# A gated recurrence and a gated linear unit on one core: roots of the first chunks on VectorE, decay constants by a series, and a new order of the queues

## The chip, the core and the metric

The kernel runs on one core of a Trainium2 chip. The core has five engines that run their own queues of instructions: TensorE (PE; its weight loads are shown as PEld), VectorE (DVE), ScalarE (ACT), GpSimd (POOL) and SyncE (SP), which here issues nearly all DMA transfers. The metric is the time of one execution on the device, in microseconds (us).

## The reference

Inputs `x`, `r_gate` and `i_gate` have the shape (4, 6336, 256). First comes a gated linear recurrence along the 6336 steps of each of 4 sequences, then a gated linear unit with a causal convolution of 5 taps:

```python
a_base = sigmoid(a_param)                                   # 256 values
a_t = exp(8 * sigmoid(r_gate) * log(clip(a_base, 1e-6, 1 - 1e-6)))
norm = sqrt(maximum(1 - a_t * a_t, 1e-6))
x_gated = norm * sigmoid(i_gate) * x
h = a_t[:, t] * h + x_gated[:, t]                           # for every t; y[:, t] = h
gate = sigmoid(sum over k of conv_w[k] * y shifted by 4 - k)
out = (gate * (y @ w_val)) @ w_out
```

## The kernel before

The 25,344 rows are cut into 51 windows of 512 rows (the first two and the last have 256), and the windows into 28 chunks: chunks 0, 1 and 2 are single windows of 256, 256 and 512 rows, chunks 3 to 25 have two windows of 512, the last two are single again. Everything is unrolled in Python. Nothing is scheduled by a compiler: a string, `ORDER`, lists some 980 steps, and each step appends its instructions to the queues of its engines in that order. A step is a name with a window or chunk number, a half of the 256 columns where it has one, and PSUM banks after `@`. Within one engine the instructions run in the order of the string; between engines semaphores make an instruction wait for its data and for its buffers.

The steps of the recurrence, by chunk `c`, half `h` or window `w`:

- `lr.w`, `li.w`, `lx.w`: SP issues the load of a window of `r_gate`, `i_gate` or `x` into a ring of four windows. A load waits until the step that reads the old content of its place is done.
- `ta.c`, `tb.c`: ACT takes tanh of half the gate (a sigmoid is taken as half of one plus tanh), into `taring` and `tbring`.
- `tr.c.h`: PE transposes the tangents of `r_gate` to PSUM; `ex.c.h`: ACT takes the exponential with scale and bias from `khf`, 128 x 2 constants worked out at the start, and writes the decays to `aring`. From chunk 3 on one `tr` and one `ex` do two chunks.
- `sq.c.h`: POOL squares the decays into `ering` (`sa` does the same on ACT for a few).
- `rt.b.k`: ACT takes the root of a quarter less a quarter of the square, for a batch `b` of chunks, as bfloat16 in place. The root is in another set of ACT's tables than tanh and exp, so a batch is framed by two table loads.
- `pp.w`, `up.w`: POOL adds one to the tangent of the input gate and multiplies by `x`, into `uring`. For a few windows `xp.w` (PE copies `x` to PSUM) and `uv.w` (DVE does both in one operation) take their place.
- `nt.c`: PE transposes the roots' packed words; `xg.c`: DVE multiplies them with `uring`; `xt.c.h`: PE transposes the product; `sc.c.h`: DVE scans, with the decays from `aring`, into `yring`.

The steps of the second layer, by window: `cv.w` (PE, the convolution as products with diagonal matrices), `tg.w` (ACT, tanh for its gate), `vl.w` (PE, product with `w_val`), `gv.w` (DVE, gate times value), `ou.w` (PE, product with `w_out`), `cd.w` or `ca.w` (copy from PSUM by DVE or ACT), `st.w` (SP, store).

Ahead of them stand `s_ident` (an identity matrix), `s_small` (loads of `a_param` and `conv_w`), `s_kt` (the constants `khf`), `s_diag` (the diagonal matrices), and among them `s_wl` and `s_wcast` (the weights). In `s_kt` ACT takes an exponential, DVE makes the clipped sigmoid of it in three operations (lines 228 to 230), ACT takes its logarithm (line 232), loads another set of tables (line 233), and DVE multiplies by four (line 234). The tables with the logarithm are loaded first of all (line 185).

The lists that the change touches besides: `BATCHES` says which chunks' roots are taken together, and the dispatch loop loads a set of tables where a step needs another one than is loaded:

```python
table, have = {"ta": EXP, "tb": EXP, "tg": EXP, "ex": EXP, "rt": SQRT}, EXP
for word in ORDER.split():
    ...
    if table.get(name, have) != have:
        have = table[name]
        nc.scalar.preload_act_table_set(have)
    emit[name](*[int(k) for k in idx], *[int(k) for k in at.split(",") if k])
```

Of the kernel before, what the change touches and what calls it, by code (L numbers as in the profile page):

```python
# [8 lines left out]
P = 128  # L9
CONV_K = 5  # L10
FP32 = mybir.dt.float32
BF16 = mybir.dt.bfloat16
ACT = mybir.ActivationFunctionType
ALU = mybir.AluOpType
# [4 lines left out]
BATCHES = [[0, 1, 2], [3, 4], [5, 6, 7, 8], [9, 10, 11, 12], [13, 14, 15, 16], [17, 18, 19, 20], [21, 22, 23, 24], [25,  # L19
    26, 27]]  # L20
# [21 lines left out]
s_ident s_small s_kt s_diag lr.1 lr.0 lr.2 lr.3 li.0 ta.0 ta.1 lr.4 tr.0.1@0 tr.0.0@7 ex.0.1 lr.5 tr.1.0@3 ta.2 ex.1.0  # L42
lr.6 tr.2.0@2 ex.0.0 li.2 sq.1.0 ex.2.0 tr.1.1@7 li.1 tr.2.1@6 ex.1.1 lx.0 tb.0 s_wl.1 ta.3 li.4 pp.0 li.3 sq.0.1 lx.1
sq.2.0 ex.2.1 lr.7 ta.4 lr.8 lx.2 tb.2 tr.3.0@0,1 s_wl.3 up.0 lr.10 tb.1 sq.2.1 ex.3.0 tr.3.1@6,7 lx.3 sq.0.0 lx.4
ex.3.1 sq.3.0 s_wl.2 s_wl.0 tb.3 sq.1.1 xp.1@7 sq.4.0 ta.5 li.8 uv.1 lr.9 sq.4.1 li.5 li.6 xp.2@4,5 sq.3.1 uv.2 rt.0.0
lx.6 pp.3 li.7 rt.1.0 lr.12 nt.1@2 pp.4 nt.0@7 xg.1 xg.0 xt.0.0@6 up.4 xt.0.1@1 nt.2@7 sc.0.0 xt.1.0@2 xt.1.1@4 sc.0.1
xg.2 up.3 lx.8 sc.1.1 nt.3@6,7 lx.5 sc.1.0 lr.11 xt.2.0@4 ta.6 cv.1@2,3 sc.2.0 s_wcast cv.0@0,1 xg.3 xt.2.1@4 tg.0
lr.14 tb.4 lr.13 sc.2.1 xt.3.0@7 lx.7 vl.0@0,1 gv.0 tb.5 li.10 pp.6 sc.3.0 tr.5.0@0,1 up.6 tg.1 ex.5.0 vl.1@4,5 gv.1
pp.5 tr.5.1@6,7 sq.5.0 ou.0.0@4 ex.5.1 cv.2@2,3 cd.0.0 st.0 xt.3.1@4 up.5 li.11 tg.2 li.12 sc.3.1 vl.2@0,1 li.9 ta.7
ou.1.0@3 pp.7 nt.4@6,7 cd.1.0 cv.3@4,5 ta.8 up.7 xg.4 st.1 lx.9 lx.10 gv.2 tg.3 tr.7.1@2,3 lr.18 sq.5.1 xt.4.1@7 lr.15  # L50
ex.7.1 xt.4.0@6 lr.16 sc.4.1 tr.7.0@0,1 sq.6.1 cv.4@4,5 ex.7.0 sc.4.0 sq.7.1 xp.8@2,3 tg.4 lx.12 lx.11 tb.6 uv.8
vl.4@0,1 sq.8.0 ou.2.0@4,5 gv.4 cv.5@6,7 tb.7 li.14 sq.6.0 lr.17 cd.2.0 li.13 vl.5@2,3 tg.5 li.15 sq.8.1 li.16 xp.9@0,1
gv.5 st.2 uv.9 sq.7.0 rt.2.0 ou.4.0@2,3 cd.4.0 ou.5.0@4,5 pp.11 cd.5.0 xp.10@6,7 up.11 lx.14 uv.10 lx.13 rt.2.1
vl.3@2,3 gv.3 nt.5@4,5 pp.12 lx.15 xg.5 nt.6@0,1 up.12 xg.6 xt.5.0@7 xt.5.1@2 sc.5.0 cv.6@4,5 tb.8 ou.3.0@0,1 ta.10
li.18 cd.3.0 pp.13 pp.14 sc.5.1 ta.9 lr.22 nt.7@0,1 up.14 lr.21 xt.6.1@7 tb.9 sc.6.1 lr.19 tr.9.0@2,3 lr.20 up.13 li.17
lx.16 tg.6 st.3 xg.7 vl.6@6,7 li.19 ex.9.0 pp.15 li.20 tr.9.1@4,5 gv.6 st.4 xt.6.0@0 up.15 xt.7.0@1 sc.6.0 ex.9.1
ou.6.0@2,3 pp.16 ta.12 cv.7@4,5 sc.7.0 sq.10.0 cv.9@6,7 tg.7 lr.25 st.5 sq.9.1 cd.6.0 tg.9 lx.18 nt.8@0,1 lr.26 ta.11
xg.8 vl.7@4,5 up.16 xt.7.1@7 gv.7 cv.8@2,3 tb.10 lr.24 lr.23 sc.7.1 sq.9.0 lx.20 ou.7.0@0,1 tg.8 tr.11.0@4,5 ex.11.0
pp.18 cd.7.0 vl.8@6,7 cv.10@2,3 sq.10.1 gv.8 st.7 li.22 tg.10 st.6 vl.9@0,1 lx.17 pp.17 tb.11 gv.9 ou.8.0@6,7
tr.11.1@4,5 cd.8.0 xt.8.0@1 ex.11.1 pp.19 sc.8.0 st.8 ou.9.0@2,3 lx.19 sq.11.0 cv.12@6,7 li.21 ta.14 xt.8.1@4 sq.11.1  # L60
sc.8.1 cv.11@0,1 tg.12 tg.11 up.18 cd.9.0 ta.13 vl.11@4,5 gv.11 vl.10@6,7 pp.20 lx.22 lr.30 vl.12@0,1 gv.10 sq.12.0
li.24 lr.27 rt.3.0 gv.12 lr.28 ou.11.0@6,7 sq.12.1 cd.11.0 ou.10.0@0,1 cd.10.0 ou.12.0@2,3 up.17 rt.3.1 cd.12.0
nt.9@6,7 xg.9 up.19 lx.21 nt.10@0,1 lr.29 xg.10 li.23 xt.9.0@5 st.10 st.9 up.20 sc.9.0 st.11 nt.11@6,7 xt.10.1@0 tb.12
tr.13.1@2,3 xg.11 xt.9.1@1 cv.13@4,5 ex.13.1 li.25 pp.22 sc.9.1 li.26 up.22 vl.13@6,7 tg.13 sc.10.1 cv.15@2,3 ta.15
sq.13.1 cv.14@4,5 tg.15 lr.31 gv.13 lr.32 pp.21 tg.14 vl.15@0,1 lx.24 gv.15 sq.14.1 vl.14@2,3 tb.13 tr.13.0@6,7 gv.14
# [43 lines left out]
def kernel(  # L109
# [30 lines left out]
    clen = [sum(CHUNKS[c]) for c in range(NCH)]  # L140
# [5 lines left out]
    e_at = SQUARES_AT  # L146
# [35 lines left out]
    live = {}  # L182
# [391 lines left out]
```

## Time and profile before

| | before |
|---|---|
| time, median of 3 runs (us) | 285.6 (285.45 to 285.82) |
| time of the profiled execution (us) | 285.77 |
| its span, first to last instruction (us) | 284.0 |
| granted clock of TensorE, mean | 0.985 |
| ACT, DVE, PE, POOL busy (us) | 270.3, 245.4, 240.4, 235.3 |
| moved by DMA | 104.75 MB, 369 GB/s over the span |

The time of an execution holds 1.8 us outside of the span. In the profile a row of a group has the busy time in us, the mean length of one instruction in ns, and the idle time of the engine just before the group with what ended most of it. A row of the timeline begins with its start and length in us; an arrow in brackets names the idle time before it and the releaser. L366 is line 366 of the kernel.

### The profile page before, as it was taken

What the parts mean: (1) busy time and instruction counts of PE and PEld (TensorE: products, weight loads), DVE (VectorE), ACT (ScalarE), POOL (GpSimd) and SP (SyncE); (2) the same over time, 40 slices, a digit from 0 to 9 for tenths busy, and PEclk for the clock granted to TensorE, in tenths of its full rate; (3) what the DMA queues carried; (4) which work ended last, traced back from release to release, by engine and by line L of the source; (5) the groups of instructions that cost most, each with busy time, mean ns of one, the idle gap of its engine ahead of it and who ended that gap; (6) DMA issues with size and microseconds to landing.
All of it is one profiled execution on the core that took longest, in us unless ns stands there. A gap on an engine that the chain in (4) does not pass through costs nothing.

```text
span 284.0 us, 6202 instructions
## 1 busy us (share of the span) xinstructions
PE 240.4 (85%) x2468; PEld 163.3 (58%) x2491; DVE 245.4 (86%) x203; ACT 270.3 (95%) x192; POOL 235.3 (83%) x157
## 2 busy tenths in 40 slices
PE   2247779997789889999898998899998989999993
PEld 1232556555656557584476584666774756856662
DVE  2002887989999999999999999999999999999981
ACT  6899999999999999999999999999999999998763
POOL 1369989997999998999999999998998997993200
PEclk9995999999999999999999999999999999999998
DMA  7999999999999999999999999999999999772646
GB/s 235 360 401 377 408 410 412 408 411 404 313 387 420 416 419 409 414 414 413 418 420 414 412 413 412 417 413 415 411 321 366 392 420 364 277 259 108 250 178 247
DMA packets 29995, 104.75 MB, mean 369 GB/s; under 512 B 3335, under 2 KB 3854, under 8 KB 29966
## 3 DMA queue, kind: packets, MB, share of 16 engines
q1 hardware_dynamic: 29952, 104.35, 94.0%
q8 instruction: 19, 0.31, 0.4%
q14 instruction: 10, 0.08, 0.1%
q10 hardware_dynamic: 14, 0.01, 0.0%
HBM read 78.39 MB, written 25.95 MB: 367 GB/s over the span
## 4 chain that ended last, share of the span: by engine, by line
ACT 29%; PE 19%; POOL 18%; DMA 11%; DVE 11%; issue 10%; SPq 0%; ACTq 0%; DVEq 0%; POOLq 0%
POOL ering L366 8%; DVE yring L463 7%; ACT taring L295 7%; ACT aring L358 7%; POOL uring L317 7%; ACT tbring L298 6%; PE banks L475 6%; PE banks L490 5%; DMA iring<-in_i_gate_dram 5%; DMA xring<-in_x_dram 4%; ACT tgring L482 4%; PE banks L505 3%; POOL tbring L305 3%; ACT oring L515 3%; DMA rring<-in_r_gate_dram 2%
## 5 line engine op out<-in xcount | busy, mean ns | idle before, releaser
L366 POOL TENSOR_TENSOR ering<-aring 128x1024 f32<-128x1024 f32 (+2 forms) x54 | 91.0, 1705 | 11.5 <-ACT aring L358 11.3
L463 DVE TENSOR_TENSOR_SCAN yring<-aring,yring,banks 128x1024 bf16<-128x1024 f32 (+5 forms) x48 | 98.4, 2060 | 2.2 <-PE banks L430 1.9
L317 POOL TENSOR_TENSOR uring<-tbring,xring 128x1024 bf16<-128x1024 bf16 (+1 forms) x46 | 96.7, 2115 | 4.3 <-DMA xring<-in_x_dram 3.3
L475 PE MATMUL banks<-yring,diag 64*64 64x512 bf16 (+7 forms) x1080 | 62.6, 361 | 2.5 <-ACT aring L358 0.9
L495 DVE SCALAR_TENSOR_TENSOR tgring<-tgring,banks 128x1024 bf16<-128x1024 bf16 (+1 forms) x51 | 59.1, 1178 | 4.8 <-PE banks L490 2.3
L305 POOL TENSOR_SCALAR tbring<-tbring 128x1024 bf16<-128x1024 bf16 (+1 forms) x46 | 46.9, 1030 | 17.2 <-ACT tbring L298 17.2
L505 PE MATMUL banks<-wo,tgring 128*128 128x256 bf16 x396 | 51.5, 273 | 5.1 <-DVE tgring L495 2.9
L490 PE MATMUL banks<-yring,wv 128*128 128x512 bf16 (+4 forms) x193 | 48.4, 359 | 6.1 <-DVE yring L463 2.5
L358 ACT ACTIVATE aring<-banks,khf 128x2048 f32<-128x2048 bf16 (+3 forms) x34 | 53.2, 1605 | 0.0
L505 PEld LDWEIGHTS <-tgring 128*128 128x128 bf16 x396 | 42.0, 114 | 17.0 <-issue 10.0
L482 ACT ACTIVATE tgring<-banks 128x1024 bf16<-128x1024 f32 (+1 forms) x51 | 50.6, 1009 | 0.9 <-PE banks L475 0.7
L295 ACT ACTIVATE taring<-rring 128x2048 bf16<-128x2048 f32 (+2 forms) x28 | 47.9, 1723 | 1.7 <-DMA rring<-in_r_gate_dram 1.6
L298 ACT ACTIVATE tbring<-iring 128x2048 bf16<-128x2048 f32 (+2 forms) x28 | 48.0, 1724 | 0.0
L391 ACT ACTIVATE ering<-ering 128x4096 bf16<-128x4096 f32 (+2 forms) x14 | 44.4, 3216 | 0.1
L475 PEld LDWEIGHTS <-diag 64*64 64x64 bf16 x1080 | 28.6, 106 | 25.8 <-issue 10.8
L513 DVE COPY oring<-banks 128x1024 f32<-128x1024 f32 (+1 forms) x34 | 39.7, 1180 | 0.9 <-PE banks L505 0.9
L342 PE MATMUL banks<-ident_b,taring 128*128 128x128 bf16 x396 | 30.0, 230 | 12.0 <-ACT taring L295 9.5
L342 PEld LDWEIGHTS <-taring 128*128 128x128 bf16 x396 | 25.9, 103 | 16.8 <-ACT taring L295 11.0
L490 PEld LDWEIGHTS <-wv 128*128 128x128 bf16 x216 | 19.7, 97 | 26.2 <-issue 12.7
L430 PE MATMUL banks<-ident,uring 128*128 128x128 f32 x198 | 30.0, 279 | 3.2 <-DVE uring L416 1.7
L405 PE MATMUL banks<-ident,ering 128*128 128x128 f32 x184 | 26.8, 292 | 3.3 <-ACT ering L391 1.8
L416 DVE TENSOR_TENSOR uring<-banks,uring 128x2048 bf16<-128x2048 bf16 (+2 forms) x25 | 27.9, 1128 | 0.8 <-PE banks L405 0.3
(39 smaller groups left out, 135.4 us busy)
## 6 DMA issues: line engine op xcount, KB each, us to landing
rring<-in_r_gate_dram SPq DMA_DIRECT2D x48, 512.0 KB, 8.9
iring<-in_i_gate_dram SPq DMA_DIRECT2D x48, 512.0 KB, 9.5
xring<-in_x_dram SPq DMA_DIRECT2D x48, 512.0 KB, 9.0
out_dram<-oring SPq DMA_DIRECT2D x48, 512.0 KB, 9.5
rring<-in_r_gate_dram SPq DMA_DIRECT2D x3, 256.0 KB, 3.2
iring<-in_i_gate_dram SPq DMA_DIRECT2D x3, 256.0 KB, 7.3
xring<-in_x_dram SPq DMA_DIRECT2D x3, 256.0 KB, 7.7
out_dram<-oring SPq DMA_DIRECT2D x3, 256.0 KB, 3.9
```

The costliest lines, as they stand in the source:

```text
L295: nc.scalar.activation(**tangent(c, taring, NTR, rring, NRI))
L298: nc.scalar.activation(**tangent(c, tbring, NTI, iring, NII))
L317: nc.gpsimd.tensor_tensor(out=u, in0=t1, in1=xt, op=ALU.mult)
L342: nc.tensor.transpose(out=bank[:, o:o + P], in_=taring[:, place(w, NTR), j, h * P:(h + 1) * P], identity=ident_b[:])
L358: nc.scalar.activation(out=dst, in_=src, func=ACT.Exp, scale=khf[:, h:h + 1], bias=khf[:, h:h + 1])
L366: nc.gpsimd.tensor_tensor(out=e, in0=a, in1=a, op=ALU.mult)
L463: nc.vector.tensor_tensor_scan(out=yring[:, h, col:col + o1 - o0], data0=aring[:, h, a_at[c] + o0:a_at[c] + o1], data1=xT[:, o0:o1], initi ...
L475: nc.tensor.matmul(out=gp[oh * 64:oh * 64 + 64, h, a:b], lhsT=diag[half * 64:half * 64 + 64, h, k, :], rhs=yring[half * 64:half * 64 + 64, ...
L482: nc.scalar.activation(out=tgring[:, w % NTG, :, 0:wins[w]], in_=live.pop(("gp", w))[:, :, 0:wins[w]], func=ACT.Tanh, scale=0.5)
L490: nc.tensor.matmul(out=val[:, m, a:b], lhsT=wv[:, hk, m * P:(m + 1) * P], rhs=yring[:, hk, col:col + b - a], start=(hk == 0), stop=(hk == ...
L495: nc.vector.scalar_tensor_tensor(out=tgring[:, w % NTG, :, 0:wins[w]], in0=tgring[:, w % NTG, :, 0:wins[w]], scalar=1.0, in1=live.pop(("va ...
L505: nc.tensor.matmul(out=ops[:, j * D:(j + 1) * D], lhsT=gv[:, hk, j:wins[w]:J], rhs=wo[:, hk, :], start=(hk == 0), stop=(hk == H - 1))
```

## The change

Three things are changed.

The roots of chunks 0 and 1 are no longer taken by ACT. A new step `rd` takes each by seven operations of VectorE on 512 fp32 values a partition (both halves of a chunk): it subtracts one, gets a first estimate of the inverse root by arithmetic on the bits, and corrects it with a polynomial. Its scratch is in two places of `oring` that are not used before the first outputs. `BATCHES` has chunks 0, 1 and 2 as batches of their own; chunk 2 stays with ACT, right before the batch of chunks 3 and 4.

The constants `khf` are worked out without a logarithm: one exponential on ACT, and a series for the logarithm in VectorE operations on 128 x 2 values. The first set of tables is the one with exp, and the second load of tables in `s_kt` is gone.

`ORDER` is new as a whole. It has the same steps but for these: `rd.0.0` and `rd.1.0` are added and the first batch's `rt` has chunk 2 alone; windows 3 and 6 go by `xp` and `uv` instead of `pp` and `up`, window 9 by `pp` and `up` instead of `xp` and `uv`; the copy of window 46 is on DVE instead of ACT; ACT squares other halves of chunks (22.1 and 27.1 instead of 22.0 and 26.0), POOL the ones left.

```diff
-BATCHES = [[0, 1, 2], [3, 4], [5, 6, 7, 8], [9, 10, 11, 12], [13, 14, 15, 16], [17, 18, 19, 20], [21, 22, 23, 24], [25,
-    26, 27]]
+BATCHES = [[0], [1], [2], [3, 4], [5, 6, 7, 8], [9, 10, 11, 12], [13, 14, 15, 16], [17, 18, 19, 20], [21, 22, 23, 24],
+    [25, 26, 27]]
...
-        nc.scalar.preload_act_table_set("natural_log_exp_and_others")
+        nc.scalar.preload_act_table_set("exp_and_others")
...
-            nc.scalar.activation(out=ksig[:], in_=kps[:, 0:H], func=ACT.Exp, scale=-1.0)
-            nc.vector.tensor_scalar(out=ksig[:], in0=ksig[:], scalar1=1.0, scalar2=None, op0=ALU.add)
-            nc.vector.reciprocal(out=ksig[:], in_=ksig[:])
-            nc.vector.tensor_scalar(out=ksig[:], in0=ksig[:], scalar1=1e-6, scalar2=1.0 - 1e-6,
+            low, p, z, q = kcol[:, 0], kcol[:, 1], kcol[:, 2], kcol[:, 3]
+            nc.vector.tensor_scalar(out=low, in0=kps[:, 0:H], scalar1=0.0, scalar2=4.0, op0=ALU.min, op1=ALU.mult)
+            nc.vector.scalar_tensor_tensor(out=p, in0=low, scalar=0.5, in1=kps[:, 0:H], op0=ALU.mult, op1=ALU.subtract)
+            nc.scalar.activation(out=p, in_=p, func=ACT.Exp)
+            nc.vector.tensor_scalar(out=z, in0=p, scalar1=2.0, scalar2=None, op0=ALU.add)
+            nc.vector.reciprocal(out=z, in_=z)
+            nc.vector.tensor_tensor(out=z, in0=z, in1=p, op=ALU.mult)
+            nc.vector.tensor_tensor(out=p, in0=z, in1=z, op=ALU.mult)
+            nc.vector.tensor_scalar(out=q, in0=p, scalar1=1.0 / 15, scalar2=None, op0=ALU.mult)
+            for k in (13, 11, 9, 7, 5, 3):
+                nc.vector.scalar_tensor_tensor(out=q, in0=q, scalar=1.0 / k, in1=p, op0=ALU.add, op1=ALU.mult)
+            nc.vector.scalar_tensor_tensor(out=q, in0=q, scalar=1.0, in1=z, op0=ALU.add, op1=ALU.mult)
+            nc.vector.scalar_tensor_tensor(out=q, in0=q, scalar=-8.0, in1=low, op0=ALU.mult, op1=ALU.add)
+            nc.vector.tensor_scalar(out=khf[:], in0=q, scalar1=4.0 * math.log(1e-6), scalar2=4.0 * math.log1p(-1e-6),
                                     op0=ALU.max, op1=ALU.min)
-            nc.scalar.activation(out=ksig[:], in_=ksig[:], func=ACT.Ln)
-            nc.scalar.preload_act_table_set("exp_and_others")
-            nc.vector.tensor_scalar(out=khf[:], in0=ksig[:], scalar1=4.0, scalar2=None, op0=ALU.mult)
...
+        def op_rd(b, k):
+            cs = root_pieces(b)[k]
+            o = e_at[cs[0]]
+            n = H * (e_at[cs[-1]] + clen[cs[-1]] - o)
+            v = ering[:, H * o:H * o + n]
+            y, s = (oring[:, 1].rearrange("p j d -> p (j d)")[:, j * 512:j * 512 + n] for j in range(2))
+            q = oring[:, 2].rearrange("p j d -> p (j d)")[:, 0:n]
+            nc.vector.tensor_scalar(out=v, in0=v, scalar1=-1.0, scalar2=-1e-6, op0=ALU.add, op1=ALU.min)
+            nc.vector.tensor_scalar(out=y.bitcast(I32), in0=v.bitcast(I32), scalar1=-0.5,
+                                    scalar2=float(0x5f3759df - 2 ** 30), op0=ALU.mult, op1=ALU.add)
+            nc.vector.scalar_tensor_tensor(out=s, in0=v, scalar=-5.0 / 32, in1=y, op0=ALU.mult, op1=ALU.mult)
+            nc.vector.scalar_tensor_tensor(out=y, in0=s, scalar=-32.0 / 5, in1=y, op0=ALU.mult, op1=ALU.mult)
+            nc.vector.scalar_tensor_tensor(out=q, in0=y, scalar=4.2, in1=y, op0=ALU.add, op1=ALU.mult)
+            nc.vector.scalar_tensor_tensor(out=q, in0=q, scalar=7.0, in1=y, op0=ALU.add, op1=ALU.mult)
+            nc.vector.scalar_tensor_tensor(out=ering[:].bitcast(BF16)[:, 4 * o:4 * o + n], in0=q, scalar=7.0, in1=s,
+                                           op0=ALU.add, op1=ALU.mult)
...
```

The new order's first lines, up to the roots of chunks 3 and 4 and the first gate:

```
s_ident s_small s_kt s_diag lr.0 lr.1 lr.2 lr.3 li.0 li.1 ta.0 lr.4 tr.0.0@1 ex.0.0 ta.1 ta.2 lr.5 tr.1.1@5 tr.1.0@1
ex.1.1 lr.6 tr.2.0@2 ex.1.0 tr.2.1@3 li.2 ex.2.0 sq.1.0 li.3 ex.2.1 lx.0 sq.1.1 tr.0.1@2 lx.1 tb.0 rd.1.0 ex.0.1 li.4
pp.0 ta.3 sq.0.1 sq.0.0 sq.2.0 tb.1 lr.7 ta.4 lr.8 sq.2.1 lx.2 s_wl.3 rd.0.0 lx.3 tb.2 tr.3.1@2,3 s_wl.2 up.0 s_wl.1
ex.3.1 tr.3.0@4,5 lx.4 ex.3.0 sq.4.1 lr.9 nt.0@6 xp.1@7 lr.10 tb.3 sq.4.0 nt.1@0 uv.1 li.6 xg.0 s_wl.0 xg.1 ta.5
xt.0.0@4 xt.0.1@7 sq.3.0 xt.1.0@0 xt.1.1@5 sc.0.1 li.5 sc.0.0 xp.2@6,7 lx.6 sc.1.0 sq.3.1 li.7 uv.2 lx.5 rt.2.0
xp.3@2,3 pp.4 rt.3.0 nt.2@1 li.8 up.4 xg.2 sc.1.1 lr.11 xt.2.1@6 cv.0@0,1 uv.3 lr.12 s_wcast sc.2.1 nt.3@4,5 tg.0 xg.3
ta.6 ...
```

128 lines of the change are left out of this document (63 added, 65 removed).

## The prediction

> **What bounds the kernel now.** I read the page's busy times and slices first, then ScalarE's waits, then the start of the timeline.
>
> ```profile
> PE 240.4 (85%) x2468; PEld 163.3 (58%) x2491; DVE 245.4 (86%) x203; ACT 270.3 (95%) x192; POOL 235.3 (83%) x157
> DVE  2002887989999999999999999999999999999981
> ACT  6899999999999999999999999999999999998763
> POOL 1369989997999998999999999998998997993200
> ```
> ```profile
> ACT oring L515 <- PE banks L505: 5.9, 5, 2.0
> ACT taring L295 <- DMA rring<-in_r_gate_dram: 1.6, 1, 1.6
> ```
> ```profile
> 264.21 1.01 ACT L515 COPY oring<-banks 128x1024 f32<-128x1024 f32 x1 [1.98 <-PE banks L505]
> ```
>
> ACT is busy for 270.3 of 284.0 us. Its one wait for a load, 1.6 us, is at the start; its 5.9 us on PE's output products begin with the 1.98 us before 264.21. Between them it runs without a pause, so every microsecond by which ACT starts its main stretch later, or waits inside it, is a microsecond of time. DVE and POOL have their free time at the front, where the change puts its new work. So the start decides:
>
> ```profile
> 2.65 0.17 DVE L228 TENSOR_SCALAR ksig<-ksig 128x2 f32<-128x2 f32 x1 [2.65 <-ACT ksig L227]
> 2.85 0.17 DVE L229 RECIPROCAL ksig<-ksig 128x2 f32<-128x2 f32 x1
> 3.47 1.28 ACT L233 ACT_TABLE_LOAD   x1
> 4.77 1.15 ACT L295 ACTIVATE taring<-rring 128x512 bf16<-128x512 f32 x2
> 8.03 1.06 ACT L295 ACTIVATE taring<-rring 128x1024 bf16<-128x1024 f32 x1 [1.57 <-DMA rring<-in_r_gate_dram]
> 16.72 1.17 POOL L317 TENSOR_TENSOR uring<-tbring,xring 128x512 bf16<-128x512 bf16 x1 [2.80 <-DMA xring<-in_x_dram]
> 17.40 3.99 ACT L358 ACTIVATE aring<-banks,khf 128x2048 f32<-128x2048 bf16 x2
> ```
> ```profile
> 19.52 8.02 POOL L366 TENSOR_TENSOR ering<-aring 128x1024 f32<-128x1024 f32 x5
> 22.60 0.73 DVE L331 SCALAR_TENSOR_TENSOR uring<-tbring,banks 128x512 bf16<-128x512 bf16 x1 [17.58 <-PE banks L322]
> 25.00 1.28 ACT L542 ACT_TABLE_LOAD   x1
> 26.30 5.42 ACT L391 ACTIVATE ering<-ering 128x2048 bf16<-128x2048 f32 x2
> 30.33 1.26 DVE L463 TENSOR_TENSOR_SCAN yring<-aring,banks 128x256 bf16<-128x256 f32 x2 [0.41 <-PE banks L430]
> 33.03 1.91 ACT L295 ACTIVATE taring<-rring 128x2048 bf16<-128x2048 f32 x1
> ```
>
> The reader is to see: ACT leaves the load-bound part at 8.03, runs the first squares' inputs until 21.4, roots from 26.30, and is back from its tables at 33.03. DVE rests for 17.58 us before 22.60. POOL's squares end at 27.54, just ahead of the second root (28.11: the pair began at 26.30, the first takes 1.91).
>
> **Constants by a series.** What goes is one table load (1.28) and one logarithm. What comes is two small VectorE steps ahead of the exponential and fourteen behind it, each starting 0.20 after the last (2.65 to 2.85), so khf is ready at about 5.9 instead of 3.66. ACT's first exp now waits for that, and ta.1 is queued behind it: 5.9 + 0.56 + 0.61 is 7.1, still ahead of 8.03, where the next load lands. On SP the load lr.5 waits for ta.1, about 1 us later, with five transfers ahead of it. So both the saving and the delay are hidden by that load: 0. If the cover of 0.9 us went, ACT would lose what the series overran.
>
> **Start of ACT.** From 8.03 the same twelve instructions run in another order until ex.3 at 17.4. In it ta.4 comes one short instruction later, so the sixteen transposes for ex.3 (1.05, below) end later than their turn on ACT: 0.2 lost. The root of chunks 0 to 2 (2048 elements) becomes that of chunk 2 alone (1024):
>
> ```profile
> L391 ACT ACTIVATE ering<-ering 128x4096 bf16<-128x4096 f32 x11 | 39.3, 3612 | 0.1
> L391 ACT ACTIVATE ering<-ering 128x2048 bf16<-128x2048 f32 x2 | 3.8, 1910 | 0.0
> L374 ACT ACTIVATE ering<-aring 128x512 f32<-128x512 f32 x1 | 0.7, 692 | 0.0
> L513 DVE COPY oring<-banks 128x1024 f32<-128x1024 f32 x32 | 38.4, 1212 | 0.0
> ```
> ```profile
> 37.97 1.05 PE L342 MATMUL banks<-ident_b,taring 128*128 128x128 bf16 x16 [0.85 <-DVE tgring L495]
> ```
>
> (3612 − 1910) / 2048 is 0.83 ns an element, so 0.85 is saved. The table loads around roots stay fourteen. Left to itself ACT would be at its first gate tangent at 32.4, 0.65 ahead.
>
> **The seven operations, beside POOL.** No operation of DVE on two fp32 operands in SBUF runs beside POOL in the first 30 us before. The nearest rows are two such operations alone, and scans that take both operands from SBUF near the end:
>
> ```profile
> L243 DVE TENSOR_TENSOR diag<-wcol,oring 128x640 bf16<-128x640 f32 x1 | 0.8, 824 | 0.0
> L242 DVE TENSOR_TENSOR oring<-ident 128x64 f32<-128x64 f32 x1 | 0.2, 217 | 0.0
> ```
> ```profile
> 267.77 1.18 POOL L317 TENSOR_TENSOR uring<-tbring,xring 128x512 bf16<-128x512 bf16 x1
> 268.06 1.96 DVE L463 TENSOR_TENSOR_SCAN yring<-aring,yring,uring 128x512 bf16<-128x512 f32 x1
> 270.00 1.27 DVE L463 TENSOR_TENSOR_SCAN yring<-aring,yring,uring 128x512 bf16<-128x512 f32 x1
> ```
>
> (824 − 217) / 576 is 1.054 ns an element: 0.69 for 512, 0.54 of it streaming. Five of the seven have two SBUF operands; the two tensor_scalars have one, and lie between 0.42 (two elements a cycle) and 0.69; I take 0.42, the end that costs the change least. Alone, a root is 2 × 0.42 + 5 × 0.69 = 4.3, and both end at 20.4 (11.3 + 8.6 + gaps): all inside DVE's rest, at no cost.
>
> But the last rows speak against that. Of two equal scans, the one that started while POOL multiplied took 1.96 instead of 1.27, and ended 1.07 after POOL's end at 268.95: it streamed nothing until POOL was done. I take this as a turn: of POOL and a DVE operation with two SBUF operands, one waits for the other's whole instruction. The Trainium skill (SBUF — State Buffer, SBUF: two separate sides) says the same, and more: the pair of ports is an exclusive lock, held against POOL by a two-SBUF-operand or two-port operation of DVE, and the loser fully blocks. The first half agrees with the 1.96 against 1.27; that POOL waits too, no row here shows. The kernel's other DVE work reads one operand from PSUM (banks in its rows).
>
> So I work out the start with turns. POOL's lengths, and the row of a stretch whose last figure is what the DMA engines moved, in GB/s:
>
> ```profile
> L366 POOL TENSOR_TENSOR ering<-aring 128x1024 f32<-128x1024 f32 x45 | 84.5, 1894 | 2.9 <-ACT aring L358 2.8
> L366 POOL TENSOR_TENSOR ering<-aring 128x512 f32<-128x512 f32 x3 | 3.1, 1043 | 0.0
> L366 POOL TENSOR_TENSOR ering<-aring 128x256 f32<-128x256 f32 x6 | 3.7, 614 | 8.6 <-ACT aring L358 8.6
> L305 POOL TENSOR_SCALAR tbring<-tbring 128x512 bf16<-128x512 bf16 x2 | 1.2, 620 | 10.6 <-ACT tbring L298 10.6
> 10.00:20.00 10.00, 4.58 (x38) 3.78 (x37) 0.00 (x0) 9.99 (x10) 5.64 (x8) 1.00 1.00 380
> ```
>
> The slope is 1.68 ns an element, so 0.19 of each is fixed and is hidden if it had to wait. Ends of turns: rd.1.0 starts at 11.3 behind sq.1.1, two operations to 12.0; pp.0 12.4, third 13.0, sq.0.1 13.4, fourth 13.9, sq.0.0 14.4, fifth 14.9, sq.2.0 15.8, sixth 16.3, sq.2.1 17.2, seventh 17.7. Then rd.0.0: first 18.1; up.0 (its x row lies 512 KB further back, 1.3 us at 380 GB/s: 18.0) 19.1; second and third 20.1; sq.4.1 21.8, fourth 22.4, sq.4.0 24.1, fifth 24.6, sq.3.0 26.3, sixth 26.9, sq.3.1 28.6, seventh 29.1. Chunk 0's root is there at 29.1 instead of 20.4, POOL's last square at 28.6 instead of 27.1, so rt.3.0 starts 1.1 late.
>
> Who waits for that: DVE's queue is uv.1, xg.0, xg.1 and the first scans behind rd.0.0; PE's is nt.0, xp.1, nt.1, xt.0, xt.1, then xp.2, xp.3, nt.2, xt.2.1, cv.0, in that order. xp.2 needs the bank that sc.0.1 reads.
>
> ```profile
> L322 PE MATMUL banks<-xring,ident 128*128 128x512 f32 x18 | 10.6, 716 | 4.3 <-ACT aring L358 2.6 <-DMA xring<-in_x_dram 1.7
> L331 DVE SCALAR_TENSOR_TENSOR uring<-tbring,banks 128x512 bf16<-128x512 bf16 x9 | 6.3, 739 | 21.6 <-PE banks L322 21.6
> L416 DVE TENSOR_TENSOR uring<-banks,uring 128x512 bf16<-128x512 bf16 x2 | 0.9, 426 | 0.2
> L416 DVE TENSOR_TENSOR uring<-banks,uring 128x1024 bf16<-128x1024 bf16 x1 | 0.7, 665 | 0.0
> 33.52 1.29 PE L475 MATMUL banks<-yring,diag 64*64 64x256 bf16 x40 [0.20 <-DVE yring L463]
> ```
>
> From the root: nt.0 0.5, xp.1 0.7, uv.1 0.7, xg.0 0.4, xt.0 0.8 with its wait, sc.0.1 0.7: 3.8. Then xp.2 and xp.3, four at 0.72, 2.9; nt.2 0.5; xg.2 0.7; xt.2.1 0.4; cv.0 between 0.65 (half of the row, which is two windows) and 1.3 (PE has mostly rested until then); I take 1.3: 9.6 in all. So cv.0 ends at 38.7. ACT, from rt.3.0 (28.6 + 3.6 + 1.28), stands at 33.5 and waits 5.2 us for tg.0, which is now its first instruction there, ahead of ta.6 and tb.4, which have their data. Against 33.03 before, with the same set behind it, ACT is 5.7 late, and in what follows has no pause to give back.
>
> **The rest of the order.** Before each later root ACT has the same set of instructions, but for ta.27, which moves ahead of one root. The 512-wide square on ACT (0.69) becomes 256 wide: −0.2 by 0.83 ns an element. Windows 3 and 6 go by PE and DVE, window 9 no longer: two of 0.74 more on DVE, one gate step and one product fewer on POOL, all off ACT's path. In the tail one copy moves from ACT to DVE (1.21), whose slices are full there; but ACT rests up to 1.98 before its copies, and with ACT late DVE waits for it at each gate: 0, at most +0.4. New queue orders of SP move loads by a place or two: bounded by −0.3 (an earlier start of the tail) and +1.0 (one late load), I take 0.
>
> **Sum.** 5.7 − 0.2 = +5.5 on the profiled execution's 285.77, which is 291.3; it lies 0.17 above the median of 285.6, so 291.1.
>
> **The rivals.** *No turns*: the port of those scans is not what these operations meet, or POOL's squares do not hold it. Then ACT gains 0.65 and 0.2, and the copy on DVE gives back up to 0.4: −0.2 to −1.2, about 284.9. For it: the order puts the squares at their undisturbed times, and DVE does rest there. Against it: the 1.96. It decides if rd.0.0 ends before about 22.8, from where cv.0 is there for ACT's 32.4. *DVE always ahead*: POOL waits until both roots are done (21.8), its two squares and its product follow (25.0), its four large squares end at 32.6; ACT's second root waits 5 us, tg.0 is at 37.5: +4.5, 289.9. *POOL always ahead*: rd.0.0 gets only POOL's pauses and ends near 37; tg.0 at 46.6 puts the time near 299. Nothing shown prefers an engine when both wait; a turn each is between them. *Part of the turn*: if POOL holds its port for half of an instruction, rd.0.0 ends near 25 and the cost is 1 to 2: 287.
>
> **How the numbers follow.** About 0.2% (0.57 us) is what can be told from no change. Turns, including DVE ahead, 288.5 to 293.6: 0.54; POOL ahead 0.07; part of the turn 0.06; no turns 0.33, of which 0.20 lies more than 0.2% below, 0.10 within it, 0.03 above. Slower is 0.54 + 0.07 + 0.06 + 0.03 = 0.70. The range leaves out POOL ahead and the lowest tenth: 284.4 to 293.6; the likeliest case alone has 288.5 to 293.6: its lower end is DVE ahead with the short cv.0 and the earlier tail, its upper end the fixed parts not hidden (nine times 0.19) and most of the late load.
>
> **What would show it.** Right: two-operand rows of rd.1.0 near 1 us instead of 0.69; rd.0.0 ending near 29; squares of 128x1024 above 1.9 us in their rows or starting late; ACT waiting for PE's cv.0 (or POOL's squares) some 5 us before its first gate tangent. Wrong: both roots done by 21, POOL's squares ending at 27, ACT with no wait after 8 us. A khf after 8.0 would show the series as wrongly hidden.

## The result, and the profile after

The changed kernel takes 294.11 us (median, 293.99 to 294.44) where the kernel before takes 285.71 beside it: a ratio of 1.0289, interval 1.0264 to 1.0315. The forecast was 291.1, with 284.4 to 293.6: right in sign and in kind, but too small, and the measured time lies just above the range. All of the loss lies ahead of 42 us.

First the page: busy times, slices of DVE, ACT and POOL, and the granted clock.

```profile
span 292.2 us, 6270 instructions
PE 243.3 (83%) x2495; PEld 165.7 (57%) x2495; DVE 266.8 (91%) x232; ACT 266.4 (91%) x189; POOL 237.6 (81%) x155
DVE  4499578878999999999999999999999999999991
ACT  3997629999999999999999999999999999999654
POOL 1589706999799899899999999998999995994300
PEclk9996599999999999999999999999999999999998
```

ACT has 3.9 us less work than before, and the span is 8.2 us longer. Its slices show where: 7, 6 and 2 tenths in the fourth to sixth (22 to 44 us), full from there on. ACT's waits name the partner (a line gives the total in us, the number of waits and the longest), and the timeline of ACT gives the places.

```profile
ACT tgring L512 <- PE banks L505: 10.6, 2, 7.7
ACT oring L545 <- PE banks L535: 3.7, 5, 2.0
ACT ering L400 <- POOL ering L375: 1.5, 1, 1.5
```
```profile
26.69 1.06 ACT L400 ACTIVATE ering<-ering 128x1024 bf16<-128x1024 f32 x1
29.22 3.62 ACT L400 ACTIVATE ering<-ering 128x4096 bf16<-128x4096 f32 x1 [1.47 <-POOL ering L375]
32.85 1.28 ACT L572 ACT_TABLE_LOAD   x1
41.80 0.60 ACT L512 ACTIVATE tgring<-banks 128x512 bf16<-128x512 f32 x1 [7.66 <-PE banks L505]
```

The reader is to see two waits: 1.47 us for POOL's squares, and 7.66 us for the convolution of window 0. (The other 2.9 of the 10.6 is one wait near the end, at 282.23; ACT's waits for PE's output products, 5.9 before, are 3.7.) The main stretch, which began at 33.03 before, begins at 41.80, which is 8.77 later. From there to the end it is 250.4 us, before 251.0: nothing more is lost.

Why those two come late stands in DVE's and POOL's timelines (roots of chunk 1 from 11.34, of chunk 0 from 18.10):

```profile
11.34 0.43 DVE L414 TENSOR_SCALAR ering<-ering 128x512 f32<-128x512 f32 x1 [3.81 <-POOL ering L375]
14.30 0.99 DVE L419 SCALAR_TENSOR_TENSOR oring<-oring 128x512 f32<-128x512 f32 x1
18.54 1.27 DVE L415 TENSOR_SCALAR oring<-ering 128x512 int32<-128x512 int32 x1
19.85 0.69 DVE L417 SCALAR_TENSOR_TENSOR oring<-ering,oring 128x512 f32<-128x512 f32 x1
20.57 2.27 DVE L418 SCALAR_TENSOR_TENSOR oring<-oring 128x512 f32<-128x512 f32 x1
27.47 2.26 DVE L421 SCALAR_TENSOR_TENSOR ering<-oring 128x512 bf16<-128x512 f32 x1
19.91 9.28 POOL L375 TENSOR_TENSOR ering<-aring 128x1024 f32<-128x1024 f32 x4 [0.38 <-ACT aring L367]
```

Of operations of one kind and size, 0.69 is the length alone, 0.99 beside small squares and 2.27 beside large ones; POOL's four large squares take 2.32 each (9.28 / 4) instead of 1.89. Each engine's row holds the other's turn. Last, PE (a record is one entry of the trace, and a copy of 512 columns of `x` leaves two) from chunk 0's root (29.73, the end of the row at 27.47) to window 0's convolution:

```profile
29.88 0.66 PE L435 MATMUL banks<-ident,ering 128*128 128x128 f32 x2 [10.43 <-DVE ering L421]
30.33 1.91 PE L331 MATMUL banks<-xring,ident 128*128 128x512 f32 x2
34.42 4.97 PE L331 MATMUL banks<-xring,ident 128*128 128x512 f32 x8
39.22 0.63 PE L435 MATMUL banks<-ident,ering 128*128 128x128 f32 x4
41.00 0.74 PE L505 MATMUL banks<-yring,diag 64*64 64x256 bf16 x20
```

This is the chain of which the prediction made 9.6 us; it took 12.07 (29.73 to 41.80). The copies of `x` (L331) take 1.91 and 4.97 of it.

### The profile page after: what moved, and what is told of

Its sections match the earlier page's. It is cut to its first block, busy times and chain, and to the rows that moved or that the text cites. A ratio compares the mean times of both kernels' runs of the same rounds, so it can differ in the third digit from the quotient of the medians.

```text
span 292.2 us, 6270 instructions
## 1 busy us (share of the span) xinstructions
PE 243.3 (83%) x2495; PEld 165.7 (57%) x2495; DVE 266.8 (91%) x232; ACT 266.4 (91%) x189; POOL 237.6 (81%) x155
## 4 chain that ended last, share of the span: by engine, by line
ACT 23%; PE 22%; issue 16%; DVE 15%; POOL 15%; DMA 8%; ACTq 0%; DVEq 0%; POOLq 0%; SPq 0%
POOL ering L375 7%; PE banks L505 6%; PE banks L535 5%; ACT tbring L307 5%; DVE yring L493 5%; PE banks L520 5%; POOL uring L326 5%; ACT ering L400 5%; DMA out_dram<-oring 4%; ACT aring L367 4%; DVE tgring L525 4%; ACT tgring L512 3%; DVE oring L543 3%; ACT taring L304 3%; DMA iring<-in_i_gate_dram 3%
## 5 line engine op out<-in xcount | busy, mean ns | idle before, releaser
L375 POOL TENSOR_TENSOR ering<-aring 128x1024 f32<-128x1024 f32 (+2 forms) x54 | 94.8, 1777 | 13.2 <-ACT aring L367 13.2
L326 POOL TENSOR_TENSOR uring<-tbring,xring 128x1024 bf16<-128x1024 bf16 (+1 forms) x45 | 94.8, 2121 | 1.3 <-DMA xring<-in_x_dram 0.5
L512 ACT ACTIVATE tgring<-banks 128x1024 bf16<-128x1024 f32 (+1 forms) x51 | 50.7, 1010 | 11.0 <-PE banks L505 10.6
L520 PE MATMUL banks<-yring,wv 128*128 128x512 bf16 (+4 forms) x216 | 49.3, 361 | 0.9 <-ACT aring L367 0.6
L505 PEld LDWEIGHTS <-diag 64*64 64x64 bf16 x1080 | 30.5, 106 | 26.9 <-issue 12.7
L400 ACT ACTIVATE ering<-ering 128x4096 bf16<-128x4096 f32 (+3 forms) x14 | 43.6, 3157 | 1.5 <-POOL ering L375 1.5
L543 DVE COPY oring<-banks 128x1024 f32<-128x1024 f32 (+1 forms) x35 | 40.6, 1180 | 1.4 <-PE banks L535 0.8
L460 PE MATMUL banks<-ident,uring 128*128 128x128 f32 x198 | 30.9, 282 | 6.4 <-DVE uring L446 4.2
L435 PEld LDWEIGHTS banks<-ident,ering 128*128 128x128 f32 x184 | 23.9, 208 | 18.0 <-POOL ering L375 10.7
```

The source lines that it names most:

```text
L326: nc.gpsimd.tensor_tensor(out=u, in0=t1, in1=xt, op=ALU.mult)
L375: nc.gpsimd.tensor_tensor(out=e, in0=a, in1=a, op=ALU.mult)
L400: nc.scalar.activation(out=ering[:].bitcast(BF16)[:, 4 * o:4 * o + 2 * n], in_=ering[:, 2 * o:2 * o + 2 * n], func=ACT.Sqrt, scale=-0.25, ...
L505: nc.tensor.matmul(out=gp[oh * 64:oh * 64 + 64, h, a:b], lhsT=diag[half * 64:half * 64 + 64, h, k, :], rhs=yring[half * 64:half * 64 + 64, ...
L512: nc.scalar.activation(out=tgring[:, w % NTG, :, 0:wins[w]], in_=live.pop(("gp", w))[:, :, 0:wins[w]], func=ACT.Tanh, scale=0.5)
L520: nc.tensor.matmul(out=val[:, m, a:b], lhsT=wv[:, hk, m * P:(m + 1) * P], rhs=yring[:, hk, col:col + b - a], start=(hk == 0), stop=(hk == ...
```

## The experiments

The theory at the start: DVE's operations and POOL's squares exclude each other, which makes chunk 0's root late, and behind the root stand PE's copies of `x`. Ratios are against the kernel before, run beside each.

### The turns: no operation with two SBUF operands

The scratch moves, so that each operation reads one operand from PSUM; the square of the estimate is written twice, so that there are eight operations instead of seven.

```diff
+ w, s, yp = banks[:, 6, 0:n], banks[:, 7, 0:n], banks[:, 0, 0:n]
- nc.vector.tensor_scalar(out=v, in0=v, scalar1=-1.0, scalar2=-1e-6, ...)
+ nc.vector.tensor_scalar(out=w, in0=v, scalar1=-1.0, scalar2=-1e-6, ...)
- nc.vector.scalar_tensor_tensor(out=y, in0=s, scalar=-32.0 / 5, in1=y, ...)
+ nc.vector.scalar_tensor_tensor(out=yp, in0=s, scalar=-32.0 / 5, in1=y, ...)
+ nc.vector.scalar_tensor_tensor(out=ys, in0=s, scalar=-32.0 / 5, in1=y, ...)
  ...
```

> The changed kernel, with the scratch of rd placed so that no operation has two operands in SBUF (one is in PSUM each time; an eighth operation writes one value to both memories). Turns with POOL: the operations last about 0.73 each whatever POOL does, POOL's squares of 128x1024 go back from 2.34 to 1.89 and end at 27.2 to 27.5, rd.0.0 ends near 23.4 instead of 29.7, the first gate tangent starts near 35.5 instead of 41.8, and the time falls by about 6, to 287 to 289. If the new order as such is slow (rival): 293 to 294, and the first gate tangent stays near 41. If the number of VectorE operations is what costs (rival): above 294, as there is one more.

Measured: 286.51 us, ratio 1.0002 (0.9973 to 1.0031), 0.5 below the expected 287. Its timeline, DVE and POOL, then PE and ACT:

```profile
17.66 0.70 DVE L418 SCALAR_TENSOR_TENSOR banks<-banks,oring 128x512 f32<-128x512 f32 x1
21.17 0.69 DVE L423 SCALAR_TENSOR_TENSOR ering<-oring,banks 128x512 bf16<-128x512 f32 x1
19.71 7.54 POOL L375 TENSOR_TENSOR ering<-aring 128x1024 f32<-128x1024 f32 x4 [0.72 <-ACT aring L367]
26.55 5.90 PE L331 MATMUL banks<-xring,ident 128*128 128x512 f32 x8
34.86 0.60 ACT L514 ACTIVATE tgring<-banks 128x512 bf16<-128x512 f32 x1 [2.51 <-PE banks L507]
```

Every operation takes 0.68 to 0.70, whatever POOL does; the squares are back at 1.89 (7.54 / 4); chunk 0's root is there at 21.86 instead of 29.73. So the turns are shown, and the operand's place is what makes them. But ACT still waits 2.51 us at the gate, for a chain of 13.0 (21.86 to 34.86): with the turns gone, the time is no better than before.

### Two operations of seven

```diff
- y, s = (...); q = ...
- (seven operations)
+ nc.vector.tensor_scalar(out=y, in0=v, scalar1=-0.25, scalar2=0.5, op0=ALU.mult, op1=ALU.add)
+ nc.vector.tensor_scalar(out=ering[:].bitcast(BF16)[...], in0=y, scalar1=1.0, scalar2=0.0, ...)
```

> The changed kernel with two of the seven operations of rd left, both with one operand; the other five are left out, and with them the root's value for chunks 0 and 1. Turns: rd.0.0 ends near 16, POOL's squares at 27.2 to 27.5, the first gate tangent starts at 32.4 to 33.5, and the time is 284.5 to 286. If the new order as such is slow: 290 or more.

This kernel leaves out the roots' values for two chunks; only its times are of use. Measured: 285.31 us, ratio 0.9984 (0.9957 to 1.001), the first gate tangent at 32.17 without a wait. The timeline has the two operations alone and beside POOL:

```profile
11.12 0.43 DVE L412 TENSOR_SCALAR oring<-ering 128x512 f32<-128x512 f32 x1 [4.28 <-POOL ering L375]
13.66 1.25 DVE L412 TENSOR_SCALAR oring<-ering 128x512 f32<-128x512 f32 x1 [1.66 <-POOL ering L375]
```

An operation with a single SBUF operand, but from SBUF to SBUF at 0.43 us, takes turns too. With an early root the wait at the first gate is gone, and the kernel stands within the interval of before: this front has little to win.

### The new order with ACT's roots

```diff
- BATCHES = [[0], [1], [2], [3, 4], ...
+ BATCHES = [[0, 1, 2], [3, 4], ...
  ORDER:  rd.1.0, rd.0.0 and rt.2.0 taken out; tb.3 ta.5 rt.0.0 ahead of nt.0
```

> The changed kernel's order, but the roots of chunks 0 to 2 by ACT in one batch as before, and none of the seven operations. Theory (the new order has the copies of x between the first root and the first gate, and so needs the early root of chunk 0): the root is done near 28.6, POOL's squares end at 27.0 to 27.5, the first gate tangent comes at 38.5 to 41, with a wait of 4 to 7 us, and the time is 290.5 to 293.5, nearly the changed kernel's, without any of the seven operations. Rival (the order costs nothing by itself and all of the loss is the turns): first gate tangent before 34.5, time within 1 us of before.

Measured: 292.64 us, ratio 1.022 (1.0174 to 1.0267), the tangent after a wait of 7.20. Its timeline of PE, from the batch's root on:

```profile
28.46 0.66 PE L443 MATMUL banks<-ident,ering 128*128 128x128 f32 x2 [9.30 <-ACT ering L408]
28.91 1.91 PE L339 MATMUL banks<-xring,ident 128*128 128x512 f32 x2
32.94 4.97 PE L339 MATMUL banks<-xring,ident 128*128 128x512 f32 x8
```

Without any operation of DVE on the roots the new order loses nearly the same, since its copies of `x` stand behind the first root, and the root comes at 28.3. The new order needs the early root; the turns take it away.

### The copies moved ahead of the root

The changed kernel, then the one with the scratch in PSUM, both with this order on PE (xp.3 goes behind window 0's convolution):

```diff
- nt.0@6 xp.1@7 nt.1@0 ... xp.2@6,7 ... xp.3@2,3 nt.2@1 ... xt.2.1@6 cv.0@0,1 ...
+ xp.1@7 xp.2@0,1 nt.0@6 nt.1@2 ... nt.2@6 cv.0@0,1 ... xt.2.1@7 xp.3@2,3 ...
```

> The changed kernel with another order of PE's first steps alone: the copies of x for windows 1 and 2 ahead of chunk 0's transposes, the convolution of window 0 ahead of the copy for window 3, and uv.3 behind sc.2.1; banks to suit. The roots and POOL's turns stay: rd.0.0 ends near 29.7, squares last 2.34. If the part of the delay that the forecast missed (about 3 us between chunk 0's root and the first gate) is the copies of x ahead of that gate on a slow clock: the first gate tangent starts at 36 to 37.5 instead of 41.8, and the time falls by 4 to 5, to 289 to 290. If the wait is for the scans instead: 293 to 294.

> Both edits together: scratch of rd in PSUM, and the copies of x first. Turns, with the copies as the second term: ACT has no wait over 0.5 us before the first gate tangent, which starts at 32.4 to 33.5, and the time is 284.5 to 286, within 0.3% of the kernel before. If something else in the new order is slow: 288 or more.

Measured: 292.37 us, ratio 1.0199 (1.0149 to 1.0249), and 288.98 us, ratio 1.0097 (1.0062 to 1.0132). Both miss what was expected, by 2.4 and 3.0 us. The waits of ACT, first kernel and second, then PE in the second:

```profile
ACT tgring L520 <- PE banks L513: 6.4, 2, 3.4
```
```profile
ACT tgring L522 <- PE banks L515: 8.1, 3, 3.3
```
```profile
22.54 5.49 PE L339 MATMUL banks<-xring,ident 128*128 128x512 f32 x6 [3.32 <-DVE ering L431]
34.53 3.62 PE L339 MATMUL banks<-xring,ident 128*128 128x512 f32 x4
```

With the scratch in PSUM the copies could not go ahead: they wait for the root to release its banks (22.54, behind DVE's L431) and then hold up `nt.0`. And xp.3, 3.62 us at 34.53, now stands ahead of window 1's convolution, for which ACT waits instead: 3.35 us in the second kernel, with 1.82 left at the first gate, and 3.43 in the first (2.9 of each total above is the wait near the end). The trace of the first kernel shows where the wait lies, not how much its median loses: it is of the quickest of four executions, 289.88 us, in which chunk 0's root was done at 27.46, one turn earlier than in the changed kernel, and the first gate tangent came at 34.18 without a wait. The wait was moved, not taken away; the amount of copying was the thing to look at.

### Fewer copies, with the turns kept

Window 3 by POOL as before, instead of PE and DVE:

```diff
- ... xp.3@2,3 pp.4 ... up.4 ... uv.3 ...
+ ... pp.3 pp.4 ... up.3 up.4 ...
```

> The changed kernel with window 3 by POOL (pp.3, up.3) as before, the seven operations left as they are, so that they go on taking turns with POOL. Theory (the term that the prediction made too small is the copies of x between chunk 0's root and the first gate): rd.0.0 ends near 29.5 as in the changed kernel, the first gate tangent comes at 38.5 to 39.0 instead of 41.8, time 290.5 to 291.5, the predicted one. Rival (the wait is set by something else between root and gate, or POOL's added product takes turns with DVE): tangent after 40.5 and time above 293.

Measured: 293.55 us, ratio 1.0242 (1.0202 to 1.0281), the tangent at 41.78. A miss of the full 2.9 us.

```profile
29.27 1.41 DVE L429 SCALAR_TENSOR_TENSOR ering<-oring 128x512 bf16<-128x512 f32 x1
35.36 3.62 PE L339 MATMUL banks<-xring,ident 128*128 128x512 f32 x4
38.78 1.06 PE L443 MATMUL banks<-ident,ering 128*128 128x128 f32 x4
```

The root ended at 30.68, 0.95 later, with one turn more: POOL's product `up.0` came just ahead of the root's first operation (17.95 and 18.10; in the changed kernel 18.13 and 18.10), and the seventh operation then met `pp.3`. The run with PE kept busy, below, has the same turn more with window 3 left on PE, so moving the window need not be its cause. And four records took 3.62 where eight had taken 4.97: a record's price isn't fixed. Two single records, of the run with the copies first and of the one with two operations, show both prices:

```profile
20.22 1.06 PE L339 MATMUL banks<-xring,ident 128*128 128x512 f32 x1
```
```profile
36.64 0.59 PE L331 MATMUL banks<-xring,ident 128*128 128x512 f32 x1
```

Two records in 1.91 follow each other by 0.85 (1.91 − 1.06), and four in 3.62 too. Eight in 4.97 begin so and go on at about half. PE had rested 10.43 us before this chain, so the new theory was that it is slow after a rest and must work for a while to be fast. The Trainium skill (TensorE: Matmul & The Clock Gate, Part 1: The HAM clock gate) says this: half the clock when idle, the full one after some 3.4 us of sustained work; start to start 426.7 and 215.7 ns for 512 columns of bf16. The fp32 records here take twice that either way, 0.853 and 0.430. The 3.4 us do not show in this chain: the faster rate came 7.3 us after its first instruction (29.88 to 37.16; last section).

### PE kept busy

A new step of plain matmuls into a bank that nobody reads, 42 of them ahead of `nt.0` in the changed kernel:

```diff
+ def op_fl(n, b):
+     for _ in range(n):
+         nc.tensor.matmul(out=banks[:, b], lhsT=ident_b[:], rhs=diag[...][:, 0:512], start=True, stop=True)
- ... nt.0@6 ...
+ ... fl.42@1 nt.0@6 ...
```

> The changed kernel with one addition: 42 matmuls of 128x512 bf16 into a bank that nobody reads, on PE between the transposes for chunk 3 (end 19.4 us) and chunk 0's root, where PE rested for 10.4 us. Theory (the copies of x are long because PE had rested: after a rest each 512-column record follows the last by 0.853 us, later by 0.430): the fillers end at 29.3 to 30.6, the two records of xp.1 take about 1.0 us instead of 1.91 and the eight of xp.2 and xp.3 3.4 to 3.6 instead of 4.97; rd.0.0 still ends near 29.7; the first gate tangent comes at 38.5 to 39.5 instead of 41.8, and the time is 291 to 292, the predicted one. Rival (0.853 is what such a copy takes in this stretch whatever PE did before): copies as in the changed kernel, tangent at 41.8 or later, time 294 or more.

Measured: 291.98 us, ratio 1.0203 (1.0176 to 1.023).

```profile
19.91 9.33 PE L449 MATMUL banks<-diag,ident_b 128*128 128x512 bf16 x40 [0.22 <-issue]
30.92 1.02 PE L339 MATMUL banks<-xring,ident 128*128 128x512 f32 x2
33.74 3.60 PE L339 MATMUL banks<-xring,ident 128*128 128x512 f32 x8
39.76 0.60 ACT L525 ACTIVATE tgring<-banks 128x512 bf16<-128x512 f32 x1 [6.27 <-PE banks L518]
```

The two records of xp.1 take 1.02 instead of 1.91, the eight take 3.60 instead of 4.97: with PE kept at work every record follows the last by 0.43. The chain from the root to the tangent is 9.23 us (30.53 to 39.76) instead of 12.07, and the time is within the expected 291 to 292, though the tangent is 0.26 later than expected here, since the root ended one turn later. This is one part of the term that failed, the rate of the copies, shown by itself.

The same with window 3 on POOL (44 matmuls), and with the scratch in PSUM (6 matmuls, window 3 by PE and DVE as in the changed kernel):

> The changed kernel with window 3 by POOL, as in the run that kept the turns, and 44 filler matmuls on PE ahead of chunk 0's root. Theory (with window 3 on POOL nothing was gained because PE then did not work long enough to reach its faster rate: four records took 3.62 us there against eight in 4.97): now four records take about 1.8 us, the first gate tangent comes at 37.5 to 39 instead of 41.8, time 290 to 291.5. Rival (the gain was eaten by POOL's added work taking turns with the root): rd.0.0 ends near 30.7 and the tangent stays after 40.5, time 293 or more.

> The kernel with the scratch in PSUM (no operation with two SBUF operands), window 3 by PE and DVE as in the changed kernel, and six such filler matmuls ahead of chunk 0's transposes, where PE rested for 2.8 us. Theory (its 2.5 us of wait at the first gate tangent were the copies of x at the rate after a rest): xp.2 and xp.3 take about 3.5 us instead of 5.9, the first gate tangent is at 32.4 to 32.6 without a wait, and the time is 0.2 to 0.4% below before, as with window 3 on POOL. Rival (the fillers come too late or too short to bring PE to its faster rate, or delay the chain): wait of 2 us or more stays, time as before or above.

Measured: 292.19 us, ratio 1.0222 (1.0197 to 1.0247), and 284.54 us, ratio 0.9971 (0.9952 to 0.999). First kernel, then second:

```profile
33.12 1.88 PE L339 MATMUL banks<-xring,ident 128*128 128x512 f32 x4
38.44 0.60 ACT L525 ACTIVATE tgring<-banks 128x512 bf16<-128x512 f32 x1 [5.59 <-PE banks L518]
```
```profile
25.43 3.60 PE L339 MATMUL banks<-xring,ident 128*128 128x512 f32 x8
32.05 0.60 ACT L527 ACTIVATE tgring<-banks 128x512 bf16<-128x512 f32 x1
```

In the first the four records take 1.88 instead of 3.62 and the tangent comes at 38.44 instead of 41.78, as expected; the median is 0.7 above what was expected all the same, and no better than with window 3 left on PE, which these few runs don't explain; the trace is of the quickest of the four, 291.32 us. In the second the wait of 2.51 is gone, and the eight records follow each other by 0.43 from the first. How much of that the six matmuls did is not settled by one trace: the next experiment shows PE fast early without any.

### Fewer copies, without the turns

Scratch in PSUM and window 3 on POOL; no added matmuls.

> The changed kernel with two edits: the seven operations' scratch placed so that none has two SBUF operands (as in the run with the scratch in PSUM), and window 3 taken by POOL (pp.3, up.3) as before instead of PE and DVE (xp.3, uv.3). Theory (what is left of the wait at the first gate tangent is the copies of x on PE between the root and the first gate): 2.9 us of copies leave the chain, the first gate tangent is at about 32.4 with no wait or one under 0.5, and the time is 284.6 to 285.4, 0.2 to 0.4% below before. Rival (the wait moves on to the next gates, as when the copies were only put in another order): the second gate tangent waits 2 us or more and the time is that of before or above.

Measured: 285.29 us, ratio 0.9964 (0.9945 to 0.9983).

```profile
22.69 0.66 PE L445 MATMUL banks<-ident,ering 128*128 128x128 f32 x2 [3.44 <-DVE ering L431]
26.86 1.88 PE L339 MATMUL banks<-xring,ident 128*128 128x512 f32 x4
32.38 0.60 ACT L522 ACTIVATE tgring<-banks 128x512 bf16<-128x512 f32 x1
```

The first gate tangent has no wait, and the second one, at 34.89, none either. Here PE was fast by 26.86 without any help, so the four records took 1.88. That part is luck as far as the runs show: up to there the chain has the same steps as with the scratch in PSUM alone, where the records still followed each other by 0.85 at 30. This kernel and the one just told of stand below both the changed kernel and the one before.

### The series alone

The constants of the changed kernel in the kernel before, nothing else; run twice.

```diff
- nc.scalar.preload_act_table_set("natural_log_exp_and_others")
+ nc.scalar.preload_act_table_set("exp_and_others")
- (exponential, three operations, logarithm, second table set, one operation)
+ (the series of the change)
```

> The kernel before with the constants by the series and nothing else: first table set exp, no logarithm's table set, order of queues as before. Theory (the series hides behind the load at 8.03): khf ready near 6.5 us as in the changed kernel, ACT's third tangent again at 8.0 to 8.1, time within 0.1% of before (285.6 to 286.1). Rival (the series delays ACT's first exp and the load queued behind it, and is part of what the change lost): ACT reaches its third tangent after 8.5 and the time is 0.5 us or more above before.

> The kernel before with the constants by the series and nothing else, once more, in more rounds. Theory (hidden: its trace had ACT's steps within 0.1 us of before from 33 us to 277 us): the interval holds 1, or its middle lies within 0.1% of 1. Rival (the 0.34% of the first run is real and comes from the series): ratio again 0.995 to 0.998 with an interval below 1.

Measured: 285.35 us, ratio 0.9966 (0.9944 to 0.9988), and 284.66 us, ratio 0.9972 (0.9945 to 0.9999). The series loses nothing: ACT's third tangent starts at 8.27 and 8.24, against 8.03, and waits there for its load, as before. But both runs are about 0.3% below before, and the theory that nothing at all would be seen missed. Where 0.3% should come from, the traces don't show: ACT reaches its main stretch at 33.14 and 33.30, later than the 33.03 before (these two executions, 285.69 and 285.9, are slower than their medians). This stays open. It also takes the merit from the two repaired kernels: they stand at 0.9964 and 0.9971, just where the series alone stands, so the roots on VectorE and the new order have added nothing that can be told from zero.

## Why the prediction was wrong, point by point

**Series for the constants: right in size, but its cover was used up.** khf was ready at 6.48 instead of 5.9, since its first step began at 3.12 and not at 2.65 to 2.85. ACT's first exp came later still, at 7.10, behind PE's transposes: the new order puts them into bank 1 (bank 7 before), which DVE reads out only behind the series, at 6.38. The third tangent came at 8.09, 0.06 later than before, right behind the second and without a wait for its load: nothing of the forecast cover of 0.9 us was left.

```profile
6.31 0.17 DVE L242 TENSOR_SCALAR khf<-kcol 128x2 f32<-128x2 f32 x1
7.10 0.56 ACT L367 ACTIVATE aring<-banks,khf 128x256 f32<-128x256 bf16 x1 [2.88 <-PE banks L351]
```

**Start of ACT and the smaller root: right.** The root of chunk 2 took 1.06, which is 0.85 less than the 1.91 of before, as worked out.

**Turns: right, in kind and nearly in size.** Chunk 1's root ended at 18.17 (forecast 17.7), chunk 0's at 29.73 (29.1), the squares at 29.19 (28.6), the second batch on ACT waited 1.47 (1.1). Of the 0.6 by which chunk 0's root was late, 0.4 came with chunk 1's root, and 0.2 is its own: an operation and a square of 1024 take 2.30 together (20.57 to 22.87 and so on), not the 0.54 + 1.68 = 2.22 of their streaming parts. The rival "no turns" is refuted: it needs 0.69 beside POOL, which only the scratch in PSUM gave. So are "DVE always ahead" and "POOL always ahead", as the two took strict turns, and "part of the turn", since the 2.30 holds both streaming parts whole.

**The chain from root to gate: this step failed.** It was forecast at 9.6 and took 12.07, which with the root's 0.6 makes the 3.1 us by which the tangent missed 38.7. Two mistakes are in the term of the copies, "xp.1 0.7" and "four at 0.72, 2.9". The count: 18 records stood in the row against nine of DVE's evictions, so a copy of 512 columns is two records, and the chain has two and eight, not one and four. The rate: 716 ns was a mean over records from 0.59 to 1.22 us long, which overlap; in a chain that begins after a rest of 10 us they follow each other by 0.85, in a busy stretch by 0.43. Measured, they took 1.91 and 4.97, 3.3 more than forecast. The count is the larger part: the row's busy time, 10.6 us for nine copies, is 1.18 a copy and would have made 5.9 of the five, and the slow rate of this chain put the last 1.0 on top. With PE kept busy they took 1.02 and 3.60, and the excess that is left then, 1.0, is the count. The forecast saw that PE would have rested, but applied it to the convolution, which took 0.74 and not 1.3: PE was fast again by then. That and other small steps gave back 0.8.

**The rest of the order: near.** Forecast −0.2, measured −0.6 (250.4 against 251.0 behind the start of the main stretch).

**The sum:** 8.77 − 0.6 = 8.2 on the profiled execution, forecast 5.7 − 0.2 = 5.5. The range ended at 293.6 because its upper end held only late loads and fixed parts; it had no bound for a copy at the slower of the two prices that its own row of 18 mixed.

## What to carry to other kernels

Work put on an idle engine is not free if its operands lie where a neighbour's do: give each VectorE operation one operand in PSUM, and the same work runs beside POOL at its full rate, even with one instruction more. Before a mean length is put into a chain, look at single rows behind a rest like the chain's own, and count the records per step. When a wait is long, take work out of its chain; putting the same work elsewhere in the order moved the wait to the next instruction twice.

## What the runs showed of the hardware

- Turns between VectorE and POOL are exact and mutual: 2.27 against 0.69 for DVE's operation, 2.32 against 1.89 for POOL's square, one each in turn. That POOL waits too, no row of before had shown. An operation with one SBUF operand and its result in SBUF, 0.43 alone, took 1.25 and 1.27 beside POOL. The two-port operation of the page that the prediction cites (the Trainium skill, SBUF — State Buffer, SBUF: two separate sides) would do that, and the half of the rule that was open, that POOL is held up in its turn, the squares' 2.32 bears out.
- Where the trace has changes of the granted clock on record, the rate of the matmuls follows it. In the changed kernel the copies were 0.85 apart up to 36.97, at a clock of 0.50, and 0.43 apart from 37.50, at 1.00 (first two rows below; the last three figures are granted clock, DMA share and GB/s); with the scratch in PSUM and window 3 on POOL the clock fell back to 0.50 from 32.76 to 36.17, and window 1's convolution took 1.28 there instead of 0.74. But ahead of the first change on record the view shows 1.00, whatever the rate: with the scratch in PSUM that change is at 31.18, and in the third row the copies were still 0.85 apart. There only the records' own lengths tell.

```profile
30.00:32.00 2.00, 2.00 (x4) 0.90 (x5) 0.00 (x0) 2.00 (x1) 1.92 (x2) 0.50 1.00 369
38.00:40.00 2.00, 1.85 (x8) 0.95 (x6) 0.54 (x2) 0.00 (x0) 0.00 (x0) 1.00 0.62 176
```
```profile
26.00:30.00 4.00, 4.00 (x9) 1.93 (x8) 2.77 (x5) 3.99 (x3) 3.92 (x3) 1.00 1.02 401
```

- How long PE must work before it is fast was not the same each time. From the chain's first instruction to the full clock it was 7.3 us in the changed kernel (29.88 to 37.16), 9.2 with the scratch in PSUM (22.00 to 31.18), and 3.2 with window 3 on POOL besides (22.69 to 25.93), with short pauses in all three. Within each trace the changes of the clock lie whole multiples of 3.41 us apart (in the changed kernel 20.09, 23.51 and 37.16), so where a chain falls on that grid is a part of it; what else sets the moment, no run here settles.
